# Batch 2's inputs queued behind the last weights, batch 1's attention begun at step 2, and every low part of w_out on VectorE

## The chip, the cores and the metric

The kernel runs on one core of a Trainium2 chip. A core has five engines that run side by side, each working through its own instructions in order: TensorE (PE in the profile, with its weight loads as PEld), VectorE (DVE), ScalarE (ACT), GpSimd (POOL) and SyncE (SP), which here only asks for DMA transfers. An engine that has to wait for another, or for a transfer, holds up all that is queued behind the waiting instruction on it. The metric is the device time of one execution in microseconds, lower is better.

## The reference

Eight batches, each with 8 heads of 576 rows of 64 elements. Attention is done twice: 32 packing queries per head attend to k and v, and then q attends to the 32 packed rows, which serve as keys and as values. The result, 4608 rows of 512, goes through a feed-forward block with a gate.

```python
p_packed = sm_attn(p, k, v)
out = sm_attn(q, p_packed, p_packed)
x = out.transpose(0, 2, 1, 3).reshape(B * S, H * D)   # 4608 x 512
h = x @ w_in                                          # 512 -> 2048
relu6 = np.clip(h + 3.0, 0.0, 6.0)
return (h * relu6 / 6.0) @ w_out                      # 2048 -> 512
```

`sm_attn` is a softmax over scaled scores. q, k, v and p are float32; w_in and w_out come as float64, so that the kernel has to make float32 of them itself.

## The kernel before

**Number form.** Large products run on pairs: a value is split into a high part (`_hi`, a rounded float32r) and a low part (`_lo`, value minus high part), and three products (high by high, high by low, low by high) make up one. The high part of w_out is ScalarE's copy in L162, its low part is the subtraction in L164, on GpSimd for blocks 8 to 12 and on VectorE for the others.

**Weights.** w_in and w_out come in 16 blocks of 128 hidden columns each, f = 0 to 15. A block of either is 512 KB. It is asked for in L125 (`raw_in`, `raw_out`; blocks 2 and 3 in `raw`), and made float32 in four operations on three engines: two passes of ScalarE (L142, L144), a shift on VectorE (L148), and an addition on GpSimd (L152), into `w_in_sb` or `x_out`. Each of raw_in, raw_out and x_out has two buffers, so a block can be asked for when the one two before it has been narrowed. A step asks for the weights four blocks ahead (`load_w(f + 4)`).

**The first batch.** Its attention comes first (`first_attention`, up to some 34 us), and its feed-forward block in `first_moe` in 16 steps, one for each f. A step has the first product (`gemm1`, L451, 12 matmuls into `ps_h`, of which there is one pair of banks), the packed matrix of the next step (`u_m0`, called m here: matmuls in L196, copy L207, subtraction L209), the gate on ScalarE (L954) and VectorE (L955), the copies of its result (gh L963, gl L965), and the second product of the step before (`gemm2`, L856, 12 matmuls). The gate of step f is the sixteen instructions of L955 in turn: step 2's is the one at 45.80 us, step 3's at 51.24, step 7's at 85.22. The first product of the next step needs the banks that the gate reads.

**Batch 1's attention in between.** `attention(1)` is a generator; `attend` takes one of its parts before a step's first product and two after its second, from step `FIRST_AHEAD` on. Its first parts ask for p and for two of four blocks of k (`nat`, two buffers, each block in four loads, L216), turn them on VectorE (L401, `tr`), and ask for the third block of k, then the fourth and v, then q, each into the buffer that a transposition frees. After k come the scores (`ps`, L268) and their copies e (L284) and maxima (L285), the exponentials (L293), the transposed weights et (L307 to L312), the product with v (L323), and the same for q.

**What sets the order.** In the first attention and in steps 0 to 3 TensorE, VectorE, ScalarE and GpSimd run in the order of the code (`manual_schedule`); from step `IN_ORDER` = 4 on a planner with its own estimates of times orders them. SyncE's queue is the planner's throughout, under the edges that `tc.issue_after` draws: it puts an instruction of the same engine behind a given one, without a wait. At most eight transfers are under way, because the queue waits for the transfer asked for eight before. All inputs and weights go through this queue.

**The later batches.** `moe(b, (c,), fill)` runs batch b in two halves of 16 steps, and `fill` takes three parts of attention(b + 1) in each step (`ahead`). So attention(2), with its loads, is traced in batch 1's steps; the planner may ask for its inputs earlier.

Of the kernel before, what the change touches and what calls it, by code (L numbers as in the profile page):

```python
# [10 lines left out]
F32 = mybir.dt.float32  # L11
# [7 lines left out]

FIRST_AHEAD = 4
PER_FIRST_STEP = (1, 2)
PER_STEP = 3


IN_ORDER = 4


POOL = range(8, 13)  # L30


WARM = (3, 2, 2, 1, 3)
# [3 lines left out]
def packed_attention_moe(  # L37
# [17 lines left out]
    nc = tc.nc  # L55
# [5 lines left out]
    NF = DF // P  # L61
# [5 lines left out]
    FPC = NB // P  # L67
# [16 lines left out]
    wo_hi = const.tile([P, NF, DM], F32R, name="wo_hi")  # L84
    wo_lo = const.tile([P, NF, DM], F32R, name="wo_lo")
# [42 lines left out]
    def narrowed(f, name):  # L128

        raw = raws.pop((name, f))
        if not wide_in:
            state["w", name, f] = raw
            return
        words = raw.rearrange("p (n two) -> p n two", two=2)  # L140
        low, high = words[:, :, 0], words[:, :, 1].bitcast(F32)
        nc.scalar.activation(out=high, in_=high, func=AF.Prelu, scale=2.0 ** -112, alpha=2.0 ** 32)  # L142
        yield
        nc.scalar.activation(out=low, in_=low.bitcast(U32), func=AF.Copy, scale=2.0 ** -29)  # L144
        yield
        x = w_in_at(f) if name == "in" else wp.tile([P, DM], F32, name="x_out")
        xi = x.bitcast(I32)
        nc.vector.tensor_scalar(  # L148
            out=xi, in0=high.bitcast(I32), scalar1=3, scalar2=None, op0=ALU.logical_shift_left
        )  # L150
        yield
        nc.gpsimd.tensor_tensor(out=xi, in0=xi, in1=low, op=ALU.add)  # L152
        state["w", name, f] = x
# [4 lines left out]
    def w_out_step(f):  # L158
        yield from narrowed(f, "out")
        yield  # L160
        x = state.pop(("w", "out", f))
        nc.scalar.copy(out=wo_hi[:, f], in_=x)  # L162
        yield
        (nc.gpsimd if f in POOL else nc.vector).tensor_sub(out=wo_lo[:, f], in0=x, in1=wo_hi[:, f].bitcast(F32))  # L164

    raws, early = {}, {}

# [12 lines left out]
    state = {}  # L180
# [206 lines left out]
    def u_m(b, n):  # L387
        hi, lo = m_tiles(b, n)
        for x, ps in enumerate(each_head(pps[b % 2], lambda a, half: w_in_sb[n][half, :, a])):
            nc.scalar.copy(out=hi[:, x], in_=ps)  # L390
            nc.vector.tensor_sub(out=lo[:, x], in0=ps, in1=hi[:, x].bitcast(F32))  # L391
# [67 lines left out]
    def first_attention():  # L459
# [287 lines left out]
        step(tq[1])  # L747
        qt.append(next(tq[1]))
        win0, wout0 = w_in_step(0), w_out_step(0)
        pv_ps = wide()  # L750
        pack(0, *et0, r0, v0)
# [6 lines left out]
        b0, b1 = s2(0), s2(1)  # L758
        m0, m1 = u_m0(0, tail), u_m0(1, tail)
        win1, wout1 = w_in_step(1), w_out_step(1)  # L760
        step(b0)
        rest(win0)
# [21 lines left out]
        step(m1, 2)  # L784
        step(wout0)
        win2, wout2 = w_in_step(2), w_out_step(2)
        step(win2, 2)
        step(wout2, 2)
# [65 lines left out]
    def second_product(f, acc, hi, lo):  # L854
        for i, (gg, ww) in enumerate(((hi, wo_hi), (hi, wo_lo), (lo, wo_hi))):
# [6 lines left out]
            )  # L862

    def moe(b, chunks, fill):

        even = b % 2 == 0
# [30 lines left out]
    def first_moe(h, w_in, w_out):  # L897
# [4 lines left out]
        def attend(f, n):  # L902
            if f >= FIRST_AHEAD:
                for _ in range(n):
                    next(ahead, None)
# [88 lines left out]
    for b in range(1, B):  # L994
        ahead = attention(b + 1) if b + 1 < B else iter(())
        late = [(b, n) for n in range(1 if b == 1 else NCH - 1, NCH)]
        soon = [(b + 1, n) for n in range(NCH - 1)] if b + 1 < B else []

        def fill(c, f):
            s = c * NF + f  # L1000
            if late:
                u_m(*late.pop(0))
            elif c == 1 and f % FPC == 0 and f >= FPC and soon:
                u_m(*soon.pop(0))
            for _ in range(PER_STEP if s < NF + FPC - 1 else 1000):
                if next(ahead, ahead) is ahead:
                    break
        for c in range(2):
            moe(b, (c,), lambda f, c=c: fill(c, f))
    with tc.manual_schedule(engines={mybir.EngineType.PE}):  # L1010
# [30 lines left out]
```

## Time and profile before

| | |
|---|---|
| median of 3 runs | 759.98 us (759.15 to 761.87) |
| the profiled execution | 758.97 us |
| its span, first to last instruction | 757.1 us |
| mean granted clock of TensorE | 0.995 |
| TensorE busy | 739.4 us, 98% of the span |
| VectorE, ScalarE, GpSimd busy | 44%, 51%, 37% |
| TensorE busy from 200 to 700 us, of 500 | 497.7 us |

The page's rows give the start, the duration and the engine with its line, then the tile written and those read, and in brackets how long the engine idled before it and who ended that. An engine's name with a q (SPq) is its instruction queue: asking for a transfer, or waiting. Busy time of TensorE counts a matmul until its modelled end. Transfers, in the view of groups, are listed with KB and the time from asking to landing.

### The profile page before, as it was taken

To read this page: it belongs to the slowest core of one execution; us is meant where nothing else is said; L and a number is where in the kernel's file an instruction comes from. 1 tells how busy PE (TensorE), PEld (TensorE's weight loads), DVE (VectorE), ACT (ScalarE), POOL (GpSimd) and SP (SyncE) were. 2 spreads that over 40 slices of the span, in tenths; PEclk is the share of its full clock that TensorE was granted. 3 is DMA by queue.
4 is the path that set the end of the run, shared out by engine and by line. 5 is a ranking of instruction groups with operands and counts; after the bars stand their busy time and mean duration, and the time that the engine had idled before them with its cause. 6 is when DMAs were issued, how large, how long until landed. Compare 5 with 4: busy or idle time off the path is not lost.

```text
span 757.1 us, 13994 instructions
## 1 busy us (share of the span) xinstructions
PE 739.4 (98%) x5197; PEld 583.4 (77%) x5197; DVE 336.3 (44%) x709; ACT 387.6 (51%) x922; POOL 282.3 (37%) x420
## 2 busy tenths in 40 slices
PE   8998898999999999999999999999999999999998
PEld 6775675768777877888777886788787887888886
DVE  3676648432463355342733446342643527321121
ACT  4677864644455446463455535463354635553343
POOL 0487973423233233332333223333333333343332
PEclk9999899999999999999999999999999999999999
DMA  9859983104420532043310524024220210000010
GB/s 257 261 144 218 237 223 63 56 9 88 102 37 29 103 67 52 1 88 71 63 43 1 114 53 82 1 58 98 47 61 1 61 33 29 1 29 0 2 42 29
DMA packets 191205, 55.98 MB, mean 74 GB/s; under 512 B 173216, under 2 KB 184480, under 8 KB 191136
## 3 DMA queue, kind: packets, MB, share of 16 engines
q1 hardware_dynamic: 191136, 55.08, 31.6%
q8 instruction: 41, 0.67, 0.4%
q14 instruction: 28, 0.23, 0.1%
HBM read 45.61 MB, written 9.44 MB: 73 GB/s over the span
## 4 chain that ended last, share of the span: by engine, by line
PE 83%; DMA 5%; DVE 4%; SPq 3%; ACT 3%; issue 1%; POOL 1%; DVEq 0%; POOLq 0%; ACTq 0%
PE acc L856 47%; PE ps_hh L827 23%; PE ps L268 6%; SPq L216 2%; DMA raw_in<-in_moe_w_in_dram 2%; PE ps L323 2%; DMA nat<-in_k_dram 1%; PE ps_h L451 1%; DVE tr L401 1%; PE ps L307 1%; SPq L254 1%; POOL x_out L152 1%; PE ps_w L639 1%; DMA raw_out<-in_moe_w_out_dram 1%; DMA spare<-in_k_dram 1%
## 5 line engine op out<-in xcount | busy, mean ns | idle before, releaser
L845 POOL TENSOR_TENSOR g<-t,g 128x256 fp32r<-128x256 f32 x224 | 167.5, 751 | 410.7 <-ACT g L844 384.5
L856 PE MATMUL acc<-wo_hi,g 128*128 128x512 f32 x896 | 316.4, 394 | 1.3 <-ACT g L844 1.3
L840 DVE SCALAR_TENSOR_TENSOR t<-t,ps_hh 128x320 f32<-128x320 f32 (+1 forms) x224 | 100.1, 449 | 251.8 <-ACT t L839 251.6
L839 ACT ACTIVATE t<-ps_hh,three 128x320 f32<-128x320 f32 (+1 forms) x224 | 112.4, 503 | 177.9 <-PE ps_hh L827 169.8
L856 PEld LDWEIGHTS acc<-wo_hi,g 128*128 128x128 f32 x896 | 167.7, 188 | 35.4 <-issue 3.5
L856 PE MATMUL acc<-wo_lo,g 128*128 128x512 f32 x448 | 177.6, 396 | 0.0
L844 ACT CAST g<-t 128x256 fp32r<-128x256 f32 x224 | 90.4, 405 | 93.9 <-DVE t L840 92.6
L827 PE MATMUL ps_hh<-a_hi,m_hi 128*128 128x320 f32 (+1 forms) x448 | 136.2, 304 | 0.3 <-DVE t L840 0.3
L827 PE MATMUL ps_hh<-a_lo,m_hi 128*128 128x320 f32 (+1 forms) x448 | 132.7, 296 | 0.0
L827 PE MATMUL ps_hh<-a_hi,m_lo 128*128 128x320 f32 (+1 forms) x448 | 132.7, 296 | 0.0
L827 PEld LDWEIGHTS ps_hh<-a_hi,m_hi 128*128 128x128 f32 x448 | 84.4, 188 | 34.4 <-issue 19.9
L856 PEld LDWEIGHTS acc<-wo_lo,g 128*128 128x128 f32 x448 | 84.5, 189 | 12.4 <-issue 2.1
L827 PEld LDWEIGHTS ps_hh<-a_lo,m_hi 128*128 128x128 f32 x448 | 84.5, 189 | 8.2 <-issue 0.9
L827 PEld LDWEIGHTS ps_hh<-a_hi,m_lo 128*128 128x128 f32 x448 | 84.5, 189 | 1.6 <-issue 1.3
L401 DVE STREAM_TRANSPOSE tr<-nat 128x576 f32<-128x576 f32 x56 | 41.8, 765 | 30.2 <-DMA nat<-in_q_dram 12.8
L391 DVE TENSOR_TENSOR m_lo<-ps,m_hi 128x512 fp32r<-128x512 f32 x56 | 36.1, 684 | 35.1 <-ACT m_hi L390 35.1
L851 POOL TENSOR_TENSOR bnd_lo<-t,bnd_hi 128x64 fp32r<-128x64 f32 x112 | 39.1, 349 | 0.0
L390 ACT CAST m_hi<-ps 128x512 fp32r<-128x512 f32 x56 | 30.0, 589 | 9.9 <-PE ps_hh L827 8.1
L268 PE MATMUL ps<-w_in_sb,pps 64*32 64x512 f32 x448 | 34.3, 601 | 0.6 <-DVE m_lo L391 0.6
L856 PE MATMUL acc<-wo_hi,gh 128*128 128x512 f32 x64 | 26.7, 417 | 2.7 <-ACT gh L963 2.7
L152 POOL TENSOR_TENSOR w_in_sb<-w_in_sb,raw_in 128x512 int32<-128x512 int32 x14 | 18.9, 1347 | 27.7 <-ACT raw_in L144 19.2
L965 POOL TENSOR_TENSOR gl<-t,gh 128x512 fp32r<-128x512 f32 x16 | 22.0, 1373 | 17.6 <-ACT bnd_hi L964 11.0
(171 smaller groups left out, 861.5 us busy)
## 6 DMA issues: line engine op xcount, KB each, us to landing
out_dram<-osb SPq DMA_DIRECT2D x36, 256.0 KB, 2.1
nat<-in_k_dram SPq DMA_DIRECT2D x112, 72.0 KB, 2.6
nat<-in_q_dram SPq DMA_DIRECT2D x112, 72.0 KB, 2.5
raw_in<-in_moe_w_in_dram SPq DMA_DIRECT2D x14, 512.0 KB, 5.6
raw_out<-in_moe_w_out_dram SPq DMA_DIRECT2D x14, 512.0 KB, 6.0
v_nat<-in_v_dram SPq DMA_DIRECT2D x56, 128.0 KB, 2.9
spare<-in_k_dram SPq DMA_DIRECT2D x2, 512.0 KB, 4.8
raw<-in_moe_w_in_dram SPq DMA_DIRECT2D x2, 512.0 KB, 4.4
```

Source lines behind the costliest of these rows:

```text
L152: nc.gpsimd.tensor_tensor(out=xi, in0=xi, in1=low, op=ALU.add)
L268: nc.tensor.matmul(banks[x][NPK * a:NPK * a + NPK, :n], rows[half, a], c, start=True, stop=True)
L390: nc.scalar.copy(out=hi[:, x], in_=ps)
L391: nc.vector.tensor_sub(out=lo[:, x], in0=ps, in1=hi[:, x].bitcast(F32))
L401: nc.vector.transpose(out=t, in_=state.pop(("nat", which, b, a)))
L827: nc.tensor.matmul(h[:, :n], mm[:, g, fs], aa[:, t0:t0 + n], start=(g == 0 and i == 0), stop=(g == NG - 1 and i == 2),)
L839: nc.scalar.activation(out=t[:, :n], in_=h, func=AF.Relu, bias=three)
L840: nc.vector.scalar_tensor_tensor(out=t[:, :n], in0=t[:, :n], scalar=6.0, in1=h, op0=ALU.min, op1=ALU.mult)
L844: nc.scalar.copy(out=gh, in_=tm)
L845: nc.gpsimd.tensor_sub(out=gl, in0=tm, in1=gh.bitcast(F32))
L851: nc.gpsimd.tensor_sub(out=bnd_lo[:, slot:slot + REM], in0=tb, in1=bh.bitcast(F32))
L856: nc.tensor.matmul(acc, gg, ww[:, f], start=(f == 0 and i == 0), stop=(f == NF - 1 and i == 2),)
```

## The change

Three edits:

- `FIRST_AHEAD` goes from 4 to 2: the parts of batch 1's attention start two steps earlier, in steps whose order on four engines is that of the code.
- The low part of w_out is VectorE's for all 16 blocks.
- In the later batches each part of `ahead` is traced under an edge behind `state["load"]`, the last weight that was asked for. On SyncE, batch 2's loads come after it.

```diff
@@ -19,15 +19,12 @@
-FIRST_AHEAD = 4
+FIRST_AHEAD = 2
 PER_FIRST_STEP = (1, 2)
 PER_STEP = 3
 IN_ORDER = 4
-POOL = range(8, 13)
 WARM = (3, 2, 2, 1, 3)
@@ -161,7 +158,7 @@
         nc.scalar.copy(out=wo_hi[:, f], in_=x)
         yield
-        (nc.gpsimd if f in POOL else nc.vector).tensor_sub(out=wo_lo[:, f], in0=x, in1=wo_hi[:, f].bitcast(F32))
+        nc.vector.tensor_sub(out=wo_lo[:, f], in0=x, in1=wo_hi[:, f].bitcast(F32))
@@ -1002,9 +999,10 @@
-            for _ in range(PER_STEP if s < NF + FPC - 1 else 1000):
-                if next(ahead, ahead) is ahead:
-                    break
+            with tc.issue_after(state["load"].ins):
+                for _ in range(PER_STEP if s < NF + FPC - 1 else 1000):
+                    if next(ahead, ahead) is ahead:
+                        break
```

Lines of the changed kernel are three lower than those of the old one up to the last edit, so L952 there is L955 here.

What this moves is seen in the order of the instructions, at three places. **VectorE at steps 2 and 3**, before: the two gates are ps_h_594 and ps_h_651, `p_tr` and `tr` are the transpositions of p and k.

```order
L955 SCALAR_TENSOR_TENSOR t<-t,ps_h_594 128x576
L209 TENSOR_TENSOR m_lo<-ps_607,m_hi 128x2x128
L164 TENSOR_TENSOR wo_lo<-x_out,wo_hi 128x512
L148 TENSOR_SCALAR x_out<-raw_out 128x512
L148 TENSOR_SCALAR w_in_sb_614<-raw_in 128x512
L955 SCALAR_TENSOR_TENSOR t<-t,ps_h_651 128x576
L244 STREAM_TRANSPOSE p_tr<-p_nat 128x128
L401 STREAM_TRANSPOSE tr<-nat 128x576 x2
```

And with the change, where the gates are ps_h_609 and ps_h_695, step 4's is ps_h_797:

```order
L952 SCALAR_TENSOR_TENSOR t<-t,ps_h_609 128x576
L206 TENSOR_TENSOR m_lo<-ps_622,m_hi 128x2x128
L161 TENSOR_TENSOR wo_lo<-x_out,wo_hi 128x512
L145 TENSOR_SCALAR x_out<-raw_out 128x512
L241 STREAM_TRANSPOSE p_tr<-p_nat 128x128
L398 STREAM_TRANSPOSE tr<-nat 128x576 x3
L145 TENSOR_SCALAR w_in_sb_629<-raw_in 128x512
L952 SCALAR_TENSOR_TENSOR t<-t,ps_h_695 128x576
L206 TENSOR_TENSOR m_lo<-ps_708,m_hi 128x2x128
L161 TENSOR_TENSOR wo_lo<-x_out,wo_hi 128x512
L145 TENSOR_SCALAR w_in_sb_629<-raw_in 128x512
L145 TENSOR_SCALAR x_out<-raw_out 128x512 x2
```

Two transpositions that stood behind step 3's gate stand ahead of it, and a third with them. The fourth of k follows the last row shown, ahead of step 4's gate.

**SyncE's queue where the last weights are asked for**, before: `nat` is k of batch 2, the second `v_nat` its v, and the first row is the weight of block 12.

```order
L125 DMA raw_in<-in_moe_w_in_dram 128x4x256
L125 DMA raw_out<-in_moe_w_out_dram 128x1024 x2
L216 DMA nat<-in_k_dram 32x18x32 x5
L254 DMA v_nat<-in_v_dram 128x4x64 x4
L254 DMA v_nat<-in_v_dram 64x4x64
L125 DMA raw_in<-in_moe_w_in_dram 128x4x256
L216 DMA nat<-in_k_dram 32x18x32 x2
L125 DMA raw_in<-in_moe_w_in_dram 128x4x256
L216 DMA nat<-in_k_dram 32x18x32
L125 DMA raw_out<-in_moe_w_out_dram 128x1024 x2
L254 DMA v_nat<-in_v_dram 128x4x64 x4
L254 DMA v_nat<-in_v_dram 64x4x64
```

With the change, earlier on the same queue, where blocks 6 to 10 are asked for (the first row is block 6 of w_in, the k here is batch 1's third and fourth block):

```order
L122 DMA raw_in<-in_moe_w_in_dram 128x4x256
L213 DMA nat<-in_k_dram 32x18x32 x6
L122 DMA raw_out<-in_moe_w_out_dram 128x1024
L213 DMA nat<-in_k_dram 32x18x32 x2
L213 DMA nat<-in_q_dram 32x18x32 x3
L122 DMA raw_in<-in_moe_w_in_dram 128x4x256
L213 DMA nat<-in_q_dram 32x18x32 x5
L122 DMA raw_in<-in_moe_w_in_dram 128x4x256
L122 DMA raw_out<-in_moe_w_out_dram 128x1024 x2
L122 DMA raw_in<-in_moe_w_in_dram 128x4x256
L213 DMA nat<-in_q_dram 32x18x32 x4
L122 DMA raw_in<-in_moe_w_in_dram 128x4x256
```

and at the last weights (the first row is blocks 13 and 14 of w_in):

```order
L122 DMA raw_in<-in_moe_w_in_dram 128x4x256 x2
L122 DMA raw_out<-in_moe_w_out_dram 128x1024 x2
L122 DMA raw_in<-in_moe_w_in_dram 128x4x256
L122 DMA raw_out<-in_moe_w_out_dram 128x1024
L233 DMA p_nat<-in_p_dram 32x4x32 x4
L213 DMA nat<-in_k_dram 32x18x32 x8
L251 DMA v_nat<-in_v_dram 128x4x64 x4
```

All of batch 2's loads now stand behind block 15 of w_out, and q's second block, the last four of the five loads of q in the earlier stretch, stands ahead of w_in's block 8.

**ScalarE ahead of step 5's gate.** Before, the two rows ahead of it (ps_h_808) narrow block 8 of w_in; block 7 of w_out is narrowed behind it:

```order
L162 CAST wo_hi<-x_out 128x512 x2
L142 ACTIVATE raw_in<-raw_in 128x512
L144 ACTIVATE raw_in<-raw_in 128x512
L954 ACTIVATE t<-ps_h_808,three 128x576
L142 ACTIVATE raw_out<-raw_out 128x512
```

With the change (ps_h_872) the rows narrow block 9 of w_in, then, behind the copies of m and the exponentials of the scores, block 10 of w_in and block 9 of w_out:

```order
L139 ACTIVATE raw_in<-raw_in 128x512
L141 ACTIVATE raw_in<-raw_in 128x512
L204 CAST m_hi<-ps_810 128x2x128
L290 ACTIVATE e,den<-e,nb 128x576 x2
L159 CAST wo_hi<-x_out 128x512
L204 CAST m_hi<-ps_885 128x2x128
L159 CAST wo_hi<-x_out 128x512
L139 ACTIVATE raw_in<-raw_in 128x512
L141 ACTIVATE raw_in<-raw_in 128x512
L139 ACTIVATE raw_out<-raw_out 128x512
L141 ACTIVATE raw_out<-raw_out 128x512
L951 ACTIVATE t<-ps_h_872,three 128x576
```

Step 5's gate has moved behind blocks 9 and 10 of w_in and behind blocks 7 to 9 of w_out, of which 7 and 8 are narrowed ahead of the rows shown.

## Prediction

> **What bounds the kernel now.** I read part 1 of the page first, then busy time by stretch, then the rows in which an engine says what it waited for.
>
> ```profile
> PE 739.4 (98%) x5197; PEld 583.4 (77%) x5197; DVE 336.3 (44%) x709; ACT 387.6 (51%) x922; POOL 282.3 (37%) x420
> ```
>
> TensorE is busy for 739.4 of 757.1 us, so 17.7 us of idle time are all that better order can remove, beside matmuls that run at a lower clock. The stretches say where that is (TensorE's busy time comes second in a row, its granted clock third from the end, then the DMA share and GB/s):
>
> ```profile
> 40.00:60.00 20.00, 19.57 (x115) 14.87 (x115) 13.81 (x22) 14.69 (x31) 17.15 (x16) 1.00 0.63 156
> 60.00:80.00 20.00, 17.23 (x108) 11.97 (x107) 14.09 (x27) 16.16 (x35) 14.62 (x14) 0.91 1.03 243
> 80.00:100.00 20.00, 17.72 (x169) 13.93 (x167) 9.68 (x18) 15.62 (x31) 17.76 (x16) 0.91 1.00 219
> 100.00:120.00 20.00, 18.00 (x129) 12.73 (x121) 11.65 (x21) 12.44 (x24) 12.03 (x10) 1.00 0.55 147
> 120.00:140.00 20.00, 19.50 (x124) 14.78 (x124) 16.67 (x29) 9.54 (x20) 7.27 (x8) 1.00 0.37 60
> ```
>
> From 60 to 140 us TensorE idles 2.77 + 2.28 + 2.00 + 0.50 = 7.55 us, and the mean clock of 0.91 in two rows takes up to 0.09 x 20 = 1.8 us each. So the first batch loses about 11 us. Its DMA share is 1.0 from 60 to 100: the transfers are the limit there, and TensorE is only starved by them. The three long waits of TensorE, and the clock behind two of them:
>
> ```profile
> 74.70 0.49 PE L856 MATMUL acc<-wo_hi,gh 128*128 128x512 f32 x1 [2.29 <-ACT gh L963]
> 85.40 1.07 PE L323 MATMUL ps<-v_nat,et 128*32 128x64 f32 x40 [2.03 <-ACT et L308]
> 120.15 1.09 PE L196 MATMUL ps<-w_in_sb,pp_bd 128*64 128x128 f32 x16 [1.75 <-DVE z L359]
> 75.00:80.00 5.00, 5.00 (x27) 3.66 (x26) 3.62 (x12) 3.79 (x10) 4.96 (x5) 0.66 1.09 320
> 85.00:90.00 5.00, 4.60 (x58) 3.84 (x59) 3.50 (x7) 4.07 (x9) 4.77 (x5) 0.66 1.07 335
> ```
>
> None of these waits is for a slow operation. Before the second, ScalarE itself had waited for a weight, with the gate and the copy et queued behind it:
>
> ```profile
> 82.85 0.68 ACT L142 ACTIVATE raw_in<-raw_in 128x512 f32<-128x512 f32 x1 [0.20 <-DMA raw_in<-in_moe_w_in_dram]
> 83.98 0.72 ACT L954 ACTIVATE t<-ps_h,three 128x576 f32<-128x576 f32 x1
> 84.60 0.58 ACT L308 COPY et<-ps 128x512 f32<-128x512 f32 x1
> 85.22 0.73 DVE L955 SCALAR_TENSOR_TENSOR t<-t,ps_h 128x576 f32<-128x576 f32 x1
> ```
>
> That is w_in's block 11 (the eighth raw_in that ScalarE narrows after block 3), and the gate is step 7's: the planner had put the narrowing of a block four steps ahead in front of it, in a queue that runs in order.
>
> **The change, part by part. Batch 2's inputs.** On SyncE's queue in the old order k and v of batch 2 stand among the last weights:
>
> ```profile
> 84.58 6.67 SPq L216 DMA_DIRECT2D nat<-in_k_dram x5
> 100.22 6.42 SPq L254 DMA_DIRECT2D v_nat<-in_v_dram x5
> 106.74 0.55 SPq L125 DMA_DIRECT2D raw_in<-in_moe_w_in_dram  x1
> 108.40 0.38 SPq L125 DMA_DIRECT2D raw_out<-in_moe_w_out_dram  x1
> DMA packets 11846, 5.50 MB, mean 229 GB/s; under 512 B 9793, under 2 KB 11332, under 8 KB 11844
> ```
>
> (The last row is the DMA view of 84 to 108 us.) Eight loads of k at 72 KB and v with 0.58 MB are 1.17 MB; at 229 GB/s they delay block 15 by 5.1 us. What waited for it is the idle time from 100 to 140 us: 2.00 + 0.50 = 2.5 us, which I take as gained. The cover for the moved loads is step 9 and later, when only they are left to load; without it batch 2's first transposition would wait.
>
> **Attention from step 2.** A step of the first batch without attention costs what lies between two gates:
>
> ```profile
> 45.80 0.76 DVE L955 SCALAR_TENSOR_TENSOR t<-t,ps_h 128x576 f32<-128x576 f32 x1 [0.27 <-ACT t L954]
> 48.73 0.41 DVE L148 TENSOR_SCALAR x_out<-raw_out 128x512 int32<-128x512 int32 x1
> 51.24 0.75 DVE L955 SCALAR_TENSOR_TENSOR t<-t,ps_h 128x576 f32<-128x576 f32 x1 [0.22 <-ACT t L954]
> 52.96 0.39 PE L856 MATMUL acc<-wo_hi,gl 128*128 128x512 f32 x1
> L401 DVE STREAM_TRANSPOSE tr<-nat 128x576 f32<-128x576 f32 x12 | 8.9, 758 | 2.3 <-DMA nat<-in_q_dram 1.6 <-DMA nat<-in_k_dram 0.6
> DMA to landing us min/median/max: 2.0/5.0/7.6
> DMA to landing us min/median/max: 3.7/6.1/8.3
> raw_in<-in_moe_w_in_dram SPq DMA_DIRECT2D x14, 512.0 KB, 5.6
> ```
>
> (Steps 2 and 3; the two landing rows are of nat and of raw_in between 25 and 120 us.) That is 5.44 us. No matmul is added or removed, so the change is worth what the waits become.
>
> *Step 3.* VectorE's new order has three transpositions ahead of step 3's gate, not two behind it. The third reads k's third block, whose buffer is free only when the first is transposed. VectorE: 49.1 (x_out's end) + 0.3 + 0.76 = 50.1; four loads asked for 0.5 us apart, to 52.05; landed after 2.0 more at best, 54.05; transposed at 54.85; one narrowing of 0.4; gate at 55.25, where it was 51.24. TensorE has finished the second product at 53.2, has one score matmul, and its next first product needs step 3's gate to free its one pair of banks, at 56.0: **a new wait of 2.5 us**. If k takes the median 5.0 us, it is 5.5.
>
> *Steps 4 and 5.* k's fourth transposition now stands behind gate 3 and two narrowings of w_out, and ends at about 59.6; only then may q's second block be asked for, and behind it on the queue weight 8, at 61.65, where it was 56.61. In the new order of ScalarE gate 5 stands behind w_in 7, 8, 9, 10 and w_out 7, 8, 9. Weight 8 lands 3.7 us later, at 65.4. From there I count loads. A weight of 512 KB (0.524 MB) takes 1.6 us at the 320 to 335 GB/s of the two 5 us rows above and 2.2 to 2.4 at the 243 and 219 GB/s of the 20 us rows, which have many small input pieces; I take 1.9, since the new stretch has fewer of these, and 0.4 for a load of q. Behind weight 8 come w_out 7 and 8, w_in 9, four loads of q, w_in 10, w_out 9: 5 x 1.9 + 1.6 = 11.1, so 76.5. ScalarE's two passes need 1.13 (82.85 to 83.98 above), the gate's first half 0.62: **gate 5 at 78.3**. In the old order the gate with the same place in attention was gate 7, at 85.22: 6.9 us later, but with two steps more done, 10.9 us of TensorE's work. So the changed kernel is **4.0 us behind** there. The 2.5 us of step 3 are in it; the rest are waits before attention's copies: the score maxima behind w_out 7 on VectorE, and m of step 5 behind w_in 9 and et behind w_out 9 on ScalarE.
>
> *Steps 6 to 9.* Gate 6 stands behind w_in 12, gate 7 behind w_out 12, gate 8 behind w_out 14. At 1.9 us a weight the last lands near 97, and TensorE's own work from step 6 to step 9 is what it was from step 8 to step 11, some 18 us from 80. The two are close: I put 0.6 us at step 7 and 1.0 at step 9, **1.6 us**. Half the clock's second loss (0.7 of some 1.7 us: 0.34 x 5) I count as gained, because part of its slow stretch will now lie in a wait.
>
> This chip's trace gates the clock after idle times of 2.29 and 2.03 us, and not after 1.75. [...]
>
> **Low parts on VectorE.** Five operations move:
>
> ```profile
> L164 DVE TENSOR_TENSOR wo_lo<-x_out,wo_hi x11: 680/1137/1731, 34.2 to 117.7; 128x512 fp32r<-128x512 f32 x11
> L164 POOL TENSOR_TENSOR wo_lo<-x_out,wo_hi x5: 1274/1278/1285, 75.7 to 96.8; 128x512 fp32r<-128x512 f32 x5
> ```
>
> GpSimd loses 5 x 1.28 = 6.4 us, VectorE gains 5 x 1.14 = 5.7 us. From 60 to 100 VectorE has 14.09 + 9.68 busy of 40 us, so there is room; none stands directly before a gate that isn't waiting for a weight anyway. I count 0, and up to 5 x 0.6 = 3 us if each fell ahead of a gate on the path.
>
> **The sum**: 4.0 (behind at gate 5) - 2.5 (block 15's wait) + 1.6 (steps 7 and 9) - 0.7 (clock) = +2.4 us. The profiled execution took 758.97, so 761.4; it lies 1.0 under the median of the runs, 759.98, so I predict **762.4 us** for the runs.
>
> **Rivals.** *Faster.* Weights land at 1.6 us each, k as fast as assumed. Gate 5 then comes 5 x 0.3 = 1.5 us sooner, the waits at steps 7 and 9 go, and both the slow stretch of the clock and block 15's wait go whole: 4.0 - 1.5 - 2.5 - 1.7 = -1.7, and -3.5 if the scores' own waits are also covered: 756.5 to 758. For it: 1.17 MB leave the stretch that is limited by DMA. The sum passes zero at about 1.75 us a weight (2.4 less 5 x 0.15 and less the 1.6 of steps 7 and 9). Against it: step 3's wait doesn't depend on the pace. *No change.* The pieces cancel, or the change does little: SyncE's rows for p, k's first half and v of batch 1 are the same rows in both orders, so its loads start no sooner at first. 759 to 762. *Much slower.* The pace is 2.3 us and k takes 5.0: gate 5 at +2.0, nine more weights to gate 8 at +0.4 each, 3.6: 768.
>
> **How the numbers follow.** About 0.3%, 2.3 us, is what a measurement of this kernel can tell from no change. Slower by more than that, from 762.3: 0.48, with the forecast at its lower edge and its own range 760.5 to 767. Within: 0.32. Faster: 0.20, since the price of five queued waits is worked out from pace alone, and any of them may be covered. The range is 756.5 to 768, from the fast pace to the slow one.
>
> **What would show it.** In the new profile: a third transposition of nat on VectorE that waits for k at about 51 to 54 us, and TensorE idle some 2.5 us until gate 3; gate 5 near 78 with ScalarE waiting for raw_out just before; no wait for raw_in or raw_out after 105 us; idle time of TensorE from 60 to 100 of 10 us or more, and next to none from 100 to 140. I am wrong if gate 5 comes before 76, or if k's third block has landed when VectorE gets to it.

## The result, and the profile after

The changed kernel takes 768.5 us (median of 6 runs, 768.2 to 771.89) against 760.03 us for the kernel before on the same chip: a ratio of 1.0122, 95% interval 1.0099 to 1.0145, so 8.5 us or 1.2% slower. The forecast was 762.4 us. Its direction was right, its size was not. The profiled execution took 768.22 us with a span of 766.4 us, 9.3 us more than the span before.

The page's first part, and busy time by stretch, of the changed kernel (columns as before: TensorE's busy time second, its granted clock third from the end):

```profile
PE 741.9 (97%) x5197; PEld 586.3 (76%) x5197; DVE 346.3 (45%) x714; ACT 388.0 (51%) x922; POOL 279.3 (36%) x415
...
40.00:60.00 20.00, 17.47 (x96) 12.70 (x97) 13.59 (x22) 14.34 (x29) 14.47 (x15) 0.93 0.76 161
60.00:80.00 20.00, 14.03 (x82) 10.81 (x81) 14.53 (x28) 14.23 (x31) 12.40 (x10) 0.76 0.89 239
80.00:100.00 20.00, 18.12 (x165) 14.32 (x165) 15.03 (x22) 17.12 (x34) 16.45 (x13) 0.80 0.94 257
100.00:120.00 20.00, 17.59 (x127) 12.13 (x126) 15.20 (x23) 11.42 (x23) 11.99 (x11) 1.00 0.62 133
120.00:140.00 20.00, 19.25 (x123) 14.21 (x122) 16.89 (x27) 9.27 (x20) 7.95 (x8) 1.00 0.28 45
```

From 40 to 140 us TensorE idles 2.53 + 5.97 + 1.88 + 2.41 + 0.75 = 13.5 us; before it was 8.0 (0.43, 2.77, 2.28, 2.00, 0.50). At half clock it works through six windows of 3.41 us instead of two, which costs, by estimate, another 7.8 us of its capacity against 3.4: half of its busy time in them, since the clock there is 0.50. The 128x288 matmuls of L448 follow each other at 0.24 us at half clock (76.31 to 78.95 us) and at 0.13 at full clock (92.26 to 93.06). Unused are 21.3 us against 11.4: a difference of 9.9 that accounts for the 9.3 of the span. From 140 to 200 us TensorE is busy for 60.00 of 60 us in both kernels, from 200 to 700 for 497.5 and 497.7 of 500: what is lost in the first batch is lost for good.

Where it idles (the four longest waits of TensorE, from its timeline):

```profile
56.84 0.37 PE L448 MATMUL ps_h<-a_hi,m_hi 128*128 128x288 f32 x1 [2.23 <-DVE t L952]
...
71.92 1.98 PE L193 MATMUL ps<-w_in_sb,pp_bd 128*64 128x128 f32 x16 [3.96 <-DVE mx L282]
75.91 0.61 PE L448 MATMUL ps_h<-a_hi,m_hi 128*128 128x288 f32 x1 [2.01 <-ACT m_hi L204]
82.10 1.45 PE L320 MATMUL ps<-v_nat,et 128*32 128x64 f32 x40 [1.88 <-ACT et L305]
```

These are the waits that the prediction named: step 3's gate (2.2 us), the score maxima behind w_out 7 (4.0), m of step 5 behind w_in 9 (2.0), et behind w_out 9 (1.9). VectorE at steps 3 and 4, and ScalarE and VectorE at gate 5:

```profile
54.95 0.78 DVE L398 STREAM_TRANSPOSE tr<-nat 128x576 f32<-128x576 f32 x1 [3.60 <-DMA nat<-in_k_dram]
55.65 0.38 DVE L145 TENSOR_SCALAR w_in_sb<-raw_in 128x512 int32<-128x512 int32 x1
55.96 0.74 DVE L952 SCALAR_TENSOR_TENSOR t<-t,ps_h 128x576 f32<-128x576 f32 x1
...
57.94 1.49 DVE L145 TENSOR_SCALAR w_in_sb<-raw_in 128x512 int32<-128x512 int32 x1
59.35 1.99 DVE L145 TENSOR_SCALAR x_out<-raw_out 128x512 int32<-128x512 int32 x2
61.26 0.77 DVE L398 STREAM_TRANSPOSE tr<-nat 128x576 f32<-128x576 f32 x1
...
74.39 0.66 ACT L139 ACTIVATE raw_in<-raw_in 128x512 f32<-128x512 f32 x1 [1.59 <-DMA raw_in<-in_moe_w_in_dram]
80.83 0.75 ACT L951 ACTIVATE t<-ps_h,three 128x576 f32<-128x576 f32 x1
81.61 0.76 DVE L952 SCALAR_TENSOR_TENSOR t<-t,ps_h 128x576 f32<-128x576 f32 x1
```

The third transposition waits 3.60 us for k's third block, as said, and gate 5 comes at 81.61 us.

In what follows a gate's time is counted from gate 2 of the same execution (46.47 us here, 45.80 before), since executions differ by up to 5 us ahead of it, whatever the edit. In the profiled executions gate 2 comes at 45.5 to 50.8 us. In e_start2 and e_after4, where it comes at 50.5 and 50.8 us, the mean granted clock from 20 to 40 us was 0.74; in the kernel before, the changed kernel, e_loads and e_low, where it comes at 45.8 to 47.5, it was 1.00. So a time of a whole execution also holds this difference, and the table below gives the time from gate 2 to the end beside it. Gate 5 of the changed kernel lies 35.1 us behind gate 2, gate 7 of the kernel before 39.4.

### The profile page after: what moved, and what is told of

Read it like the earlier page. It is cut to its first block, busy times and chain, and to the rows that moved or that the text cites. A ratio compares the mean times of both kernels' runs of the same rounds, so it can differ in the third digit from the quotient of the medians.

```text
span 766.4 us, 14000 instructions
## 1 busy us (share of the span) xinstructions
PE 741.9 (97%) x5197; PEld 586.3 (76%) x5197; DVE 346.3 (45%) x714; ACT 388.0 (51%) x922; POOL 279.3 (36%) x415
## 4 chain that ended last, share of the span: by engine, by line
PE 78%; DMA 6%; DVE 5%; SPq 4%; ACT 3%; issue 2%; POOL 1%; DVEq 0%; POOLq 0%; ACTq 0%
PE acc L853 46%; PE ps_hh L824 22%; PE ps L265 6%; DMA nat<-in_k_dram 2%; SPq L213 2%; PE ps L320 1%; DMA raw_in<-in_moe_w_in_dram 1%; DVE tr L398 1%; PE ps_h L448 1%; DMA v_nat<-in_v_dram 1%; DMA p_nat<-in_p_dram 1%; PE ps L304 1%; DMA raw_out<-in_moe_w_out_dram 1%; POOL x_out L149 1%; DVE w_in_sb L145 1%
## 5 line engine op out<-in xcount | busy, mean ns | idle before, releaser
L398 DVE STREAM_TRANSPOSE tr<-nat 128x576 f32<-128x576 f32 x56 | 41.8, 765 | 34.5 <-DMA nat<-in_q_dram 13.6
L388 DVE TENSOR_TENSOR m_lo<-ps,m_hi 128x512 fp32r<-128x512 f32 x56 | 36.1, 684 | 34.5 <-ACT m_hi L387 34.4
L448 PE MATMUL ps_h<-a_hi,m_hi 128*128 128x288 f32 x64 | 21.6, 338 | 6.4 <-DVE t L952 4.4
```

What stands on the lines that cost most here:

```text
L398: nc.vector.transpose(out=t, in_=state.pop(("nat", which, b, a)))
L448: nc.tensor.matmul(h[:, hf, :HS], mm[:, g, fs], aa[:, hf * HS:(hf + 1) * HS], start=(g == 0 and i == 0), stop=(g == NG - 1 and i == 2),)
```

## The experiments

All ratios are to the kernel before on the same chip, with 95% intervals. The last column is the span of the profiled execution less its gate 2: one execution of each kernel.

| kernel | edit | median, us | ratio | gate 2 to end, us |
|---|---|---|---|---|
| the changed kernel | all three | 768.5 | 1.0122 (1.0099 to 1.0145) | 719.9 (before: 711.3) |
| e_start2 | early start alone | 772.2 | 1.0149 (1.0108 to 1.0190) | 721.2 |
| e_loads | batch 2's inputs alone | 758.5 | 0.9980 (0.9962 to 0.9999) | 709.5 |
| e_low | low parts alone | 757.5 | 0.9972 (0.9952 to 0.9992) | 709.9 |
| e_after4 | inputs and low parts, start 4 | 759.4 | 1.0002 (0.9978 to 1.0026) | 712.5 |
| e_after3 | the same, start 3 | 764.3 | 1.0054 (1.0026 to 1.0083) | 714.2 |
| e_low5 | low parts, start 5 | 758.4 | 0.9982 (0.9958 to 1.0007) | 711.3 |
| x_fill | changed, idle time filled | 768.6 | 1.0114 (1.0072 to 1.0156) | 720.0 |
| x_hold | changed, k's third turn behind gate 3 | 768.0 | 1.0107 (1.0064 to 1.0150) | 717.9 |
| x_tie2 | changed, weights behind the gate two steps before | 765.0 | 1.0067 (1.0038 to 1.0095) | 715.6 |
| x_tie1 | changed, weights behind the gate one step before | 775.2 | 1.0190 (1.0137 to 1.0243) | 724.9 |
| x_light_a, x_light_b | changed, before: long runs in k and q | 764.2, 752.4 | 1.0056 (1.0031 to 1.0082), 0.9886 (0.9847 to 0.9925) | 715.7, 704.1 |
| n_after, n_before | changed, before: no loads of k and q | 766.6, 757.0 | 1.0067 (1.0038 to 1.0095), 0.9955 (0.9934 to 0.9977) | 715.8, 708.6 |
| x_front | x_tie2 with gates 5 and 6 ahead | 771.9 | 1.0162 (1.0117 to 1.0207) | 719.6 |
| n_front | x_front without loads of k and q | 768.4 | 1.0119 (1.0073 to 1.0165) | 717.9 |
| x_atie4, x_ltie2 | x_tie2's rule with start 4 | 760.6, 758.6 | 0.9996 (0.9976 to 1.0017), 0.9983 (0.9957 to 1.0009) | 712.0, 714.8 |

### Which of the three edits

e_start2 has of the diff only

```diff
-FIRST_AHEAD = 4
+FIRST_AHEAD = 2
```

> The kernel before with the start of batch 1's attention at step 2 alone; batch 2's inputs and the low parts of w_out stay as they were. Theory 1 (the early start alone makes the loss: step 3 waits for k's third block, gate 5 is queued on ScalarE behind w_in 9 and 10 and w_out 9, and TensorE then runs at half its clock): as the changed kernel, 766 to 771 us, gate 5 at 79 to 83 us, half clock for several windows between 70 and 90. Rival 2 (the moved loads or the low parts carry half of it or more): 760 to 764.

e_loads has only the edge `tc.issue_after(state["load"].ins)`, e_low only the low parts:

> The kernel before with batch 2's inputs behind the last weights alone. Theory 1: no loss; block 15 lands 3 to 5 us sooner, TensorE's 1.75 us wait at 120 us goes, 757.5 to 760. Rival 2 (the moved loads hurt): 762 to 766. If the wait is only replaced by another one, 759.5 to 760.5.

> The kernel before with all low parts of w_out on VectorE alone. Theory 1: within 1 us of before, 759 to 761, since no gate is behind them on the path. Rival 2 (VectorE's five more operations delay gates): 762 to 764.

e_after4 is the changed kernel with `FIRST_AHEAD = 4`:

> The changed kernel with the start of attention put back to step 4 (so: moved loads and low parts on VectorE, no early start). Theory 1: the whole loss is gone, 757 to 760. Rival 2: 762 to 766. Rival 3 (the pieces only lose together, because the early start crowds the weights and the low parts then stand ahead of gates): this kernel 759 to 761, and the one with the early start alone 762 to 765.

The early start alone loses 12.8 us by the medians (8 to 14 by the interval), a little more than was expected of it. The other two edits lose nothing: by the ratios 1.5 and 2.1 us less alone, no difference together. Whether the loss is smaller with them than with the early start alone is not shown: the intervals overlap, and from gate 2 on the two kernels take 719.9 and 721.2 us. So the early start makes all of the loss, and theory 1 holds as far as *which edit* goes; for the reason that it gives, see below.

### How the loss grows with the start

e_after3 is the changed kernel with `FIRST_AHEAD = 3`.

> The changed kernel with attention's start at step 3, between the two: no third transposition ahead of step 3's gate, and gate 5 behind w_in 7 to 10 and w_out 7, 8, 9 a step later. If each step of an earlier start puts weights later by the same amount: about half the loss, 762 to 766. If the loss has a threshold at step 3's wait for k: 758 to 761.

By the ratios the loss is 0.2 us for a start at 4, 4.1 at 3 and 9.3 at 2. Both steps cost, and it doesn't begin with the third transposition ahead of step 3's gate (e_after3 has none there). How the loss divides is less sure: the interval of e_after3 leaves it 2.0 to 6.3 us, and from gate 2 to the end the profiled executions take 712.5, 714.2 and 719.9 us, 1.7 us more for the first step and 5.7 for the second. The gate with the same place in attention is gate 7, 6 and 5 for a start at 4, 3 and 2. If attention moved with its start, it would come a step, 5.4 us, sooner each time. Counted from gate 2 it is at 38.4 (89.24 less 50.81), 34.5 (80.50 less 46.01) and 35.1 us: for the first step 3.9 of 5.4 us are had, for the second nothing, and TensorE has done a step or two fewer by then. What is not had, 1.5 and 6.0 us, is close to the 1.7 and 5.7 us above. Gates 2 and 7 of e_after4, then 2 and 6 of e_after3:

```profile
50.81 0.76 DVE L952 SCALAR_TENSOR_TENSOR t<-t,ps_h 128x576 f32<-128x576 f32 x1 [0.28 <-ACT t L951]
89.24 0.72 DVE L952 SCALAR_TENSOR_TENSOR t<-t,ps_h 128x576 f32<-128x576 f32 x1
...
46.01 0.75 DVE L952 SCALAR_TENSOR_TENSOR t<-t,ps_h 128x576 f32<-128x576 f32 x1 [0.28 <-ACT t L951]
80.50 0.73 DVE L952 SCALAR_TENSOR_TENSOR t<-t,ps_h 128x576 f32<-128x576 f32 x1
```

### The half clock

x_fill keeps the order of every queue and puts 24 products of zeros into the four idle times (`AT` gives the place in TensorE's queue and how many, the edges hold the rest):

```diff
+AT = {261: 5, 313: 10, 321: 5, 338: 4}
+            for _ in range(FILL.get(f, 0)):
+                filler.append(nc.tensor.matmul(accs[3][:, :2 * P], zeros[:, :P], zeros, start=False, stop=False))
...
+    pin(tc, filler)
```

> The changed kernel with every engine's queue held in exactly its own order, and 24 products of zeros by zeros added into the fourth acc on TensorE (0.33 us each at full clock): 5 before gemm1 of step 4, 10 before m of step 5, 5 before gemm1 of step 5, 4 before the first attention product with v. They fill the four idle times of 2.2, 4.0, 2.0 and 1.9 us, and no wait is taken away. If the half clock of 57 to 61 and 71 to 88 us is part of the loss: no half clock from 50 to 92, gate 4 1.5 us sooner, and 762 to 766 us. If the half clock only fills time in which gate 5 waits for weights anyway: 767 to 770.

The same stretches, the filler's rows and gates 2 and 5 of x_fill:

```profile
40.00:60.00 20.00, 19.61 (x119) 14.61 (x118) 13.51 (x21) 15.17 (x31) 14.38 (x14) 1.00 0.72 159
60.00:80.00 20.00, 19.04 (x115) 14.42 (x116) 14.75 (x28) 13.33 (x28) 14.42 (x12) 1.00 0.88 232
80.00:100.00 20.00, 15.85 (x152) 11.69 (x151) 16.84 (x24) 17.43 (x34) 14.26 (x12) 1.00 0.93 251
...
55.78 2.32 PE L946 MATMUL acc<-pps 128*128 128x256 f32 x10
69.49 4.58 PE L946 MATMUL acc<-pps 128*128 128x256 f32 x20
75.03 2.43 PE L946 MATMUL acc<-pps 128*128 128x256 f32 x10
81.09 1.89 PE L946 MATMUL acc<-pps 128*128 128x256 f32 x8
...
48.39 0.76 DVE L988 SCALAR_TENSOR_TENSOR t<-t,ps_h 128x576 f32<-128x576 f32 x1 [0.28 <-ACT t L987]
83.56 0.76 DVE L988 SCALAR_TENSOR_TENSOR t<-t,ps_h 128x576 f32<-128x576 f32 x1
```

The clock is full from 40 to 140 us, and nothing is gained: 768.6 us, 720.0 from gate 2 to the end (719.9 without filler), gate 5 at 35.2 us from gate 2 (35.1 without filler). The filler takes 11.2 us and the idle time from 40 to 140 us is then 9.9, together 21.1: the 21.3 of the changed kernel. So the half clock, the most visible thing in its profile, only fills time in which TensorE would have waited. The runs show no part of the loss in it.

### Step 3's wait for k

x_hold puts one part of attention from ahead of step 3's gate to behind it:

```diff
-        def attend(f, n):
+        def attend(f, n, late=0):
+            n += {6: -1, 7: 1}.get(2 * f + late, 0)
```

> The changed kernel with the part of batch 1's attention that holds k's third transposition behind the gate of step 3 instead of ahead of it (one part fewer ahead, one more behind). Step 3's gate then waits for no k: at 52 to 53.5 us, and the 2.2 us before gemm1 of step 4 go. If the loss is made by gate 5's place behind the narrowings of w_in 9, 10 and w_out 9 (which stays): 765 to 769. If step 3's wait and the half clock after it are the root: 761 to 764.

Its gates 2, 3 and 5:

```profile
47.83 0.76 DVE L953 SCALAR_TENSOR_TENSOR t<-t,ps_h 128x576 f32<-128x576 f32 x1 [0.27 <-ACT t L952]
53.29 0.75 DVE L953 SCALAR_TENSOR_TENSOR t<-t,ps_h 128x576 f32<-128x576 f32 x1 [0.24 <-ACT t L952]
82.69 0.71 DVE L953 SCALAR_TENSOR_TENSOR t<-t,ps_h 128x576 f32<-128x576 f32 x1
```

Gate 3 comes 4.0 us sooner (5.5 from gate 2, not 9.5), gate 5 doesn't (34.9), and the time is 768.0. TensorE's wait of 2.2 us is gone, and another of 2.29 us, for gh, ends at 65.05 us. So gate 5 doesn't depend on it. That the wait costs nothing is not shown as closely: the interval leaves some 4 us, and this execution takes 2.1 us less from gate 2 to the end, most of it behind gate 5.

### Weights ahead of the gates

x_tie2 queues what step f writes of the narrowing behind the gate of step f-2, on ScalarE and VectorE; x_tie1 has f-1 there:

```diff
+        def behind(f):
+            tied = ExitStack()
+            for ins in gates.get(f - 2, ()):
+                tied.enter_context(tc.issue_after(ins.ins))
+            return tied
...
-            step(in_(f + 2), 4)
+            with behind(f):
+                step(in_(f + 2), 4)
```

(and the same around the three calls for w_out).

> The changed kernel with the narrowing of w_in and w_out that the program writes at step f (blocks f+2 and f+1) queued behind the gate of step f-2 on ScalarE and VectorE, so that gate 5 stands behind blocks 7 and 8 only, no longer behind w_in 9, 10 and w_out 9. If the queue order at gate 5 makes the loss: gate 5 at 71 to 75 us and 757 to 762 us in all. If the loads set the pace and the wait only moves to a later gate: 765 to 769.

> As the kernel before it in this set, but queued behind the gate of step f-1: gate 5 stands behind block 7 alone. Queue order: gate 5 at 69 to 72 us, and 754 to 760 us if the weights, now narrowed a step later, still come in time; 760 to 766 with new waits for raw_in and raw_out at gates 7 to 12 if they do not.

x_tie2 gives back 3.5 us by the medians (4.3 from gate 2 to the end), less than a queue cause alone would; its gate 5 comes 31.2 us behind gate 2 (81.52 less 50.34), 4 us sooner. x_tie1, for which both expectations gave 766 us or less, is 6.7 us worse than the changed kernel by the medians: gate 5 hardly moves (34.2), because ScalarE's half is free of weights now and VectorE's half stands behind a transposition that waits for q:

```profile
79.17 0.74 ACT L960 ACTIVATE t<-ps_h,three 128x576 f32<-128x576 f32 x1 [2.39 <-PE ps_h L448]
81.93 0.78 DVE L398 STREAM_TRANSPOSE tr<-nat 128x576 f32<-128x576 f32 x1 [2.81 <-DMA nat<-in_q_dram]
82.63 0.72 DVE L961 SCALAR_TENSOR_TENSOR t<-t,ps_h 128x576 f32<-128x576 f32 x1
```

and weights narrowed later free their buffers later: between 76.6 and 86.0 us no weight is asked for, and its transfers are busy for 0.53 of 80 to 100 us, where the changed kernel has 0.94.

### The loads of k and q

x_light_a and x_light_b are the two kernels in their own order with k and q of batches 1 and later read in long runs:

```diff
-                    out=t[r:r + 32],
-                    in_=src[b, 2 * a + h, :, 32 * c:32 * c + 32].rearrange("(t i) j -> i t j", i=32),
+                    out=t[r:r + 32].rearrange("p t j -> p (t j)"),
+                    in_=src[b, 2 * a + h].rearrange("(x i r) d -> x i (r d)", x=2, i=32)[c],
```

> The changed kernel with every queue in its own order, but each piece of k and q of batches 1 and later read as 32 runs of 2304 bytes, not as 576 runs of 128 bytes: the same 72 KB and the same number of loads, with other elements of k and q in each place, so the attention of these batches is computed on rearranged inputs. If the stream of loads from 50 to 80 us sets gate 5: gate 5 at 76 to 79 us, 760 to 765 in all, and at most 5 us above the next kernel. If queue order and waits alone set it: gate 5 within 1 us of 81.6, and 8 to 10 us above the next kernel.

> The same edit of k and q in the kernel before, in its own order: the control for the run ahead of it. Load stream: 755 to 759, since the waits before gates 6 and 7 shrink too. Queue order alone: 758 to 761.

The DMA view of 60 to 80 us, of the changed kernel and of x_light_a:

```profile
DMA packets 9106, 4.78 MB, mean 239 GB/s; under 512 B 6634, under 2 KB 8645, under 8 KB 9103
```

```profile
DMA packets 3173, 5.03 MB, mean 251 GB/s; under 512 B 316, under 2 KB 2266, under 8 KB 3171
```

A third of the packets, and both kernels gain, 4.3 and 7.5 us; their distance doesn't shrink (11.8 us by the medians). Gate 5 is 33.8 us from gate 2, 1.3 sooner. The many small pieces cost time in either kernel and aren't the cause of the difference. Neither expectation is met; the one by queue order is nearer.

n_after and n_before don't load k and q of batch 1 at all:

```diff
+        if b == 1:
+            nc.gpsimd.memset(t, 0.5)
+            return t
```

> The changed kernel without the loads of k and q of batch 1: GpSimd fills each of their eight buffers with 0.5 in place of four loads, so batch 1's attention is computed on constants. Every other operation is there. If the place of these 32 loads among the weights makes the loss: gate 5 at 66 to 73 us, and at most 4 us above the next kernel. If the loss comes from the weights that stand ahead of the gates: still 8 us or more above the next kernel, with gate 5 waiting for raw_in or raw_out.

> The same in the kernel before: the control. Place of the loads: 752 to 756, since the waits of 2.3 and 2.0 us shrink or go. Weights ahead of the gates: 755 to 759.

The distance stays: 9.6 us by the medians, 7.3 from gate 2 to the end (8.6 with the loads). Gate 5 comes 32.3 us from gate 2 (81.16 less 48.86), with the same blocks 7 to 10 ahead of it on ScalarE. 32 loads fewer were worth 2.8 us there, since the engines that narrow the weights were full next: n_after from 60 to 80 us, and VectorE's shifts in that stretch,

```profile
60.00:80.00 20.00, 13.97 (x79) 9.79 (x79) 19.56 (x30) 16.01 (x34) 17.38 (x16) 0.75 0.70 215
...
L145 DVE TENSOR_SCALAR x_out<-raw_out x4: 827/1268/1546, 59.8 to 73.3; 128x512 int32<-128x512 int32 x4
L145 DVE TENSOR_SCALAR w_in_sb<-raw_in x4: 419/1245/1591, 63.4 to 78.3; 128x512 int32<-128x512 int32 x4
```

VectorE is busy for 19.56 of 20 us, GpSimd for 17.38 (1.7 of them fills that the edit adds), and the DMA share is down to 0.70 (14.53, 12.40 and 0.89 in the changed kernel). The place of k's and q's loads is not the cause of most of it.

### Gates 5 and 6 ahead of everything

x_front is x_tie2 with its queues held in their order but for one stretch, in which all that gates 5 and 6 need stands ahead of the narrowings of blocks 7 (w_out) and 8, on three engines. In ScalarE's queue (numbers are places in x_tie2's queue, 95 and 104 the gates, 82 to 85 and 88, 89 the narrowings; 86, 87 the copies e, 90 and 94 m):

```diff
-73 74 75 76 77 78 79 80 81 82 83 84 85 86 87 88 89 90 91 92 93 94 95 ... 104
+73 74 75 76 77 78 79 80 81 86 87 90 91 92 94 95 100 101 99 82 83 104 84 85 109 111 112 88 89 93
```

> The kernel with narrowings behind the gate of two steps before (early start, 765 us), its queues held in their order but for one stretch: on ScalarE, VectorE and GpSimd the score copies and maxima, m of steps 5 and 6, gates 5 and 6 and their halves stand ahead of the narrowings of blocks 7 (w_out) and 8, and of q's transpositions. Nothing is added or left out. Gate 5 then waits for no load: at 71 to 74 us (plus what its start is later), where it was at 81.6. If weights ahead of the gates are the whole cause: 754 to 760. If the two steps gained are lost again in waits for weights from gate 7 on, whose pace does not change: 762 to 767.

Gates 2, 5, 6 and 7 of x_front, TensorE's wait ahead of gate 7, ScalarE's queue in it, and the asking for w_out 9:

```profile
46.48 0.76 DVE L997 SCALAR_TENSOR_TENSOR t<-t,ps_h 128x576 f32<-128x576 f32 x1 [0.28 <-ACT t L996]
73.42 0.75 DVE L997 SCALAR_TENSOR_TENSOR t<-t,ps_h 128x576 f32<-128x576 f32 x1 [0.68 <-ACT t L996]
77.29 0.76 DVE L997 SCALAR_TENSOR_TENSOR t<-t,ps_h 128x576 f32<-128x576 f32 x1 [0.65 <-ACT t L996]
93.30 0.73 DVE L997 SCALAR_TENSOR_TENSOR t<-t,ps_h 128x576 f32<-128x576 f32 x1
...
91.18 1.12 PE L226 MATMUL ps<-w_in_sb,pp_bd 128*64 128x128 f32 x8 [6.74 <-ACT et L338]
...
86.21 0.65 ACT L172 ACTIVATE raw_out<-raw_out 128x512 f32<-128x512 f32 x1 [1.64 <-DMA raw_out<-in_moe_w_out_dram]
88.86 0.65 ACT L172 ACTIVATE raw_out<-raw_out 128x512 f32<-128x512 f32 x1 [0.32 <-DMA raw_out<-in_moe_w_out_dram]
90.46 0.58 ACT L338 COPY et<-ps 128x512 f32<-128x512 f32 x1
...
82.30 0.35 SPq L155 DMA_DIRECT2D raw_out<-in_moe_w_out_dram  x1
```

Gate 5 is at 26.9 us from gate 2 and gate 6 at 30.8, 8.2 and 12.2 us sooner than in the changed kernel. Then gate 7 waits: TensorE idles 6.74 us, the longest of its waits between gates 2 and 15 in any kernel here, for et behind blocks 9 and 10, and w_out 9 and 10 were only asked for at 82.3 and 83.8 us, where the changed kernel asked at 74.1 and 75.7, since the buffers come free when blocks 7 and 8 have been narrowed. Gate 7 comes 46.8 us from gate 2 (49.4 in the changed kernel, 43.0 in x_tie2), and the median is 771.9 us, above both expected ranges. The wait has moved, as the second theory had it, and it has grown. Whether the kernel is slower than the changed one is not shown: the intervals overlap, and from gate 2 to the end the two take 719.6 and 719.9 us. What x_tie2 had won is lost again.

n_front has the same order of TensorE, ScalarE and VectorE and no loads of k and q.

> The kernel with gates 5 and 6 ahead of the weights, without the loads of k and q of batch 1 (GpSimd fills the eight buffers with 0.5, so batch 1's attention is computed on constants); TensorE, ScalarE and VectorE keep their order. If weights ahead of the gates and the loads of k and q in the one queue make the loss only together: gate 7 at 82 to 88 us, and 754 to 760 in all, about the kernel before without these loads (757.0). If the pace of the weights alone sets gate 7: gate 7 at 90 us or later and 764 to 770.

TensorE's wait is nearly as long, and gate 7 follows at 89.67 (43.4 from gate 2):

```profile
89.14 1.12 PE L228 MATMUL ps<-w_in_sb,pp_bd 128*64 128x128 f32 x8 [5.71 <-ACT et L343]
```

768.4 us: the narrowed weights set gate 7 there without any loads of k and q.

### The other way, and a faster kernel

e_low5 starts attention a step later than the kernel before, and x_atie4 and x_ltie2 use x_tie2's rule with a start at step 4 (x_atie4 with batch 2's inputs moved, x_ltie2 without):

> The other way: the kernel before with all low parts of w_out on VectorE and attention's start at step 5. If fewer attention loads among the weights help: 753 to 757. If attention then ends too late for batch 1's second phase: 760 to 764.

> Moved loads and low parts on VectorE with the start at step 4, and the narrowings of a step queued behind the gate of two steps before. If the order at the gates is what costs: the waits of 2.3 and 2.0 us before gates 6 and 7 shrink, 753 to 757. If weights then come late instead: 760 to 764.

> The same queue rule in the kernel before with the low parts on VectorE and batch 2's inputs where they were. Order at the gates: 753 to 757. Weights late: 760 to 764.

Their medians are 758.4, 760.6 and 758.6, and all three intervals hold 1. The rule doesn't pay where the start is at 4: in x_ltie2 TensorE still waits 3.0 and 1.9 us at 72.6 and 84.6. The best kernel that computes the reference is e_low, by the ratio 2.1 us or 0.28% under the kernel before: its interval lies just under 1, and the gain is at the edge of what can be told from nothing.

## Why the prediction was right or wrong

**Right.** The early start was named as the edit that costs, by new waits at step 3 and ahead of gate 5; all four waits came where the prediction put them, step 3's with 2.2 us where 2.5 was given. Of its signs, the third transposition's wait and TensorE's wait at gate 3 are there, and no wait for raw_in or raw_out comes after 105 us. The low parts at 0 and no loss from the moved loads were right.

**Signs that failed.** The idle time from 60 to 100 us is 7.9 us and not 10 or more, and from 100 to 140 us it is 3.2 us and not next to none. ScalarE's last wait ahead of gate 5 was for w_in 9, at 74.4, and not for raw_out; after that its own queue kept it busy for 7.60 of 7.6 us to 82. So the reading that "the transfers are the limit there" is half of it: at gate 5, and in n_after with a DMA share of 0.70, the engines that narrow the weights were the ones that were full.

**Wrong, by term.** The sum was 4.0 - 2.5 + 1.6 - 0.7 = 2.4. Measured in the two spans it is 7.3 + 2.0 = 9.3. Two steps of the working failed about equally: gate 5 was placed 3.3 us too early, and all that follows it was put at -1.6 and is +2.0.

- *"4.0 us behind" at gate 5*: 7.3. Gate 5 came at 81.61, not 78.3. The counting of loads behind weight 8 was right (11.1 us taken; it landed at 68.5 and w_out 9 at 79.4, 10.9 us later). But weight 8 was asked for at 64.1, not at 61.65, behind q's second block, and that behind k's fourth transposition, which the prediction had end at "about 59.6" and which ran at 61.26. Three narrowings stand ahead of it, and VectorE took 1.49 and 1.99 (two) for them, not the 0.41 each of the row that I used; GpSimd was busy all that time. Of the 3.3 us, 0.67 is a later gate 2, ahead of any edit.
- *"- 2.5, block 15's wait", taken "as gained"*: not gained. The wait did go: w_out 15 landed at 107.5, 5.8 us sooner. TensorE's idle time from 100 to 140 us is 3.2 us all the same (2.41 + 0.75), where it was 2.5. The waits there are now mostly for the gates and for z. Alone (e_loads) the edit brings this idle time down to 1.5 us (0.51 + 1.00) and gained 1.5 us by the ratio, of which its interval just leaves some. A wait that ends last in the old order was priced as if the rest of the change left that stretch alone.
- *"1.6 us" at steps 7 and 9 and "- 0.7" for the clock*: behind gate 5 the deficit goes from 7.3 at gate 5 to 9.7 at gate 6 and ends at 9.3, so all that follows gate 5, block 15 included, is + 2.0, not - 1.6. Gate 6, for which I put no wait, stood behind w_in 11 and 12, and came 7.9 us after gate 5. The clock term is 0 as far as the runs show: with filler the clock is full (x_fill, 1.00 from 40 to 140 us), and neither gate 5 (35.2 us from gate 2, 35.1 without filler) nor the end (720.0, 719.9) moves.

**The rivals.** "Much slower" gave 768 for a pace of 2.3 us a weight and a late k. The number is close and the mechanism isn't the one: the pace up to gate 5 was the 1.9 assumed. "Faster" rested on 1.6 us a weight, which was not reached. On the way I held gate 5's place in ScalarE's queue to be the whole reason. x_front takes that place away, and the wait turns up at gate 7: this theory falls.

**What the runs support.** That the early start makes the loss is shown by experiment. Why it does is in part argued, as follows. From 50 to 95 us the kernel loads and narrows weights, at a pace that an earlier start of attention doesn't raise: blocks 9 and 10 land from 72 to 80 us before and from 74 to 83 us after. The planner's queues put attention's parts behind about these blocks in both, so the gate behind attention's place moves by 3.9 us for the first step and not at all for the second, and each step by which the start is earlier leaves TensorE a step fewer to do beforehand. There is nothing idle later that could take it back. This fits that the second step of the start loses more than the first, that neither the half clock, nor step 3's wait, nor k and q in the load queue make the loss by themselves, and that moving the gates moves the wait. That the pace is set by two buffers per kind and by four operations on three engines for each block is read from the profiles (the late askings of x_front, VectorE at 19.56 of 20 us in n_after). It wasn't isolated: a third buffer was not tried, and neither was an order in which all gates, not two, are placed by hand. So how much of the 8.5 us a better order could win back beyond x_tie2's 3.5 stays open.

## What to carry to other kernels

Starting a side task sooner gains only where the main engine will be idle later; where it is busy to the end, as here from 140 us on (497.5 of 500 us from 200 to 700), what an early wait costs can't be made up. When a wait is removed, look at what the queue is paced by: here the waits ahead of gates 3, 5 and 6 could each be moved, and waits for narrowed weights came back elsewhere. Before blaming a slow clock, fill the idle time: if the end doesn't move, as in x_fill (768.6 us against 768.5), the slow clock only took time in which the engine would have waited.

## What the hardware showed

**The clock is granted in windows.** In the traces of the two kernels half clock starts and ends on a grid of 3.41 us: from 75.6 to 79.1 and from 85.9 to 89.3 us before, from 57.2 to 60.6 and from 70.9 to 87.9 us in the changed kernel. The windows of the kernel before (72 to 89 us), then of e_low:

```profile
72.23:75.64 3.41, 1.12 (x5) 0.81 (x5) 3.41 (x6) 3.16 (x8) 1.72 (x2) 1.00 0.75 193
75.64:79.05 3.41, 3.41 (x20) 2.45 (x20) 2.61 (x8) 2.45 (x5) 3.41 (x5) 0.50 1.08 353
82.47:85.88 3.41, 1.38 (x40) 1.14 (x38) 2.10 (x4) 3.02 (x6) 2.99 (x3) 1.00 0.99 153
85.88:89.29 3.41, 3.41 (x32) 2.77 (x22) 2.18 (x4) 2.68 (x6) 3.41 (x4) 0.50 1.06 390
```

```profile
71.53:74.95 3.42, 2.44 (x23) 1.06 (x22) 2.07 (x3) 3.10 (x6) 2.30 (x3) 1.00 0.95 131
74.95:78.36 3.41, 1.82 (x8) 1.42 (x8) 3.41 (x5) 2.62 (x7) 2.33 (x2) 1.00 0.92 313
78.36:81.77 3.41, 2.87 (x23) 1.70 (x22) 2.28 (x10) 2.82 (x7) 2.28 (x3) 1.00 1.12 296
```

Busy for 1.12 and 1.38 of 3.41 us, and the next window is at half clock. In the changed kernel the two windows ahead of half clock were busy for 1.18 (53.8 to 57.2 us) and 0.50 (67.5 to 70.9): in the four, a share of 0.15 to 0.40. On the grids of these two traces every other window at full clock up to 700 us was followed by full clock; the least busy of them had a share of 0.52 (before, 116.6 to 120.0 us, 1.79 of 3.41), the others 0.72 or more. In e_low TensorE idles 0.98 and 1.59 us in two windows side by side, 2.44 and 1.82 are left busy, and the clock stays full.

In the changed kernel, windows at half clock that were busy for a share of 0.52 to 0.74 were followed by another at half clock, and one busy to the full ended it: half clock from 70.9 to 87.9 us. It didn't always end so: from 25 to 35 us e_start2 and e_after4 were busy for 9.92 of 10 us each, at a mean clock of 0.54 and 0.56, behind 5 us in which 3.33 and 3.73 were busy. The prediction's reading, that waits over some 2 us gate the clock and 1.75 doesn't, is wrong: in e_after4 TensorE idles 1.75 us from 75 to 80 us, at full clock, and from 80 to 85 us it is busy for 5.00 of 5 us at a mean clock of 0.66. What in a window brings the half clock was not isolated.

**VectorE beside GpSimd.** In the changed kernel the 13 shifts of a weight block (L145) that began while GpSimd was idle took 0.38 to 0.43 us. The 19 that began while an operation of GpSimd ran took 0.49 to 1.53 us, and each ended 0.28 to 0.29 us after that operation. So the shift at 79.46 us, with GpSimd idle, took 0.42 us; the one at 80.47 took 1.13, while an addition ran on GpSimd from 80.02 to 81.31, and ended 0.28 us after it. In n_after one took 1.59 us (the L145 rows above). A price for VectorE taken from a quiet row was too low where GpSimd was busy: the three shifts ahead of k's fourth transposition took 3.48 us (1.49 + 1.99), where three times 0.41 gives 1.23.
